# One conversion of 1024 columns for two neighbouring weight halves in a retention and two-layer feed-forward kernel

## The chip, the cores and the metric

The kernel runs on one core of a Trainium2 chip. The metric is the device time of one execution in microseconds; a median is taken over several executions. TensorE does the matrix products, ScalarE (ACT) and VectorE (DVE) everything elementwise, GpSimd (POOL) a little at the start, and SyncE (SP) issues nearly all transfers.

## What is computed

The reference, cut to what matters (2304 tokens, model width 512, hidden widths 1536 and 2048):

```python
scores = scale * q @ k.T
x = (scores * Dmat) @ v                      # decayed causal scores, 4 x 8 heads, 576 tokens
xn = x / sqrt(mean(x * x) + 1e-6) * rms_g    # first feed-forward block
g, val = xn @ w_gate, xn @ w_val
x = (g * sigmoid(g) * val) @ w_out
h = x @ w_in                                 # second feed-forward block
g = where(h >= 1, h, where(h <= -1, 0, (h + 1) ** 2 / 4))
out = g @ w_out2
```

## The kernel before, in words

**Three stages.** The attention stage works in chunks of 128 tokens (`scores` and `values`). The first feed-forward block follows: 36 steps (`step_a`), three blocks of 768 tokens with 12 steps of 128 hidden units each. The second block has three token blocks, each with eight front pieces (`front_b`) and a back part (`back_b`). Products are done as three matmuls on operands split into a rounded high and a low part (`split`: a ScalarE copy, then a VectorE subtraction), and each 2 by 2 block product takes seven products in place of eight, with sums of weight blocks and of token blocks made beforehand.

**The weights** come in as 64-bit numbers. `convert` (line 388) makes float32 of them. Its source is a ring of three buffers (`STAGE = 3`, laid out in line 345) in the tile `plain`; each holds one slot of 512 columns of 64 bits per partition, 512 KB, loaded by `load_slot` (line 380) on SP's queue. The three buffers lie side by side, so buffers 0 and 1 are neighbours, and 1 and 2; 2 and 0 are not. For each half of 512 columns, `convert` does a Prelu on ScalarE (upper words into the target), an Identity on ScalarE (the top byte of the lower words, with the bias `half`, into the stage buffer itself) and a scalar_tensor_tensor on VectorE that shifts and joins both; then it issues one `load_slot`, the refill of the ring. In program order both Preludes stand first, then Identity, join and refill of one half, then those of the other.

**Who calls it.** `prepare_a(s)` does a pair (gate and value weights, two slots) and then a single one (the output weights, one slot) for each of 12 steps; each is prepared one step ahead, the first two beside attention. `prepare_b` does one pair for each of 16 units (eight pieces, front and back weights) beside the steps from the 13th on that stand in `PREPARE`. After a pair comes the making of four sums on VectorE and `split_seven`, seven splits in three groups. In the 13th step and after, weights of the first block are read back from memory (`load_a`, tile `wt`; `load_out`), and those of the second are written out (`wfd`, `wod`, tile `late`) and read back later.

**The order** of the work is made by a planner (`Plan`). Every operation is recorded with its regions, a cost by a formula (`cost`), and a due time worked back from its users. `issue` then orders each engine's list: the operation ready next, and of those ready within 100 ns the one due first. TensorE keeps its program order. The order is fixed when the program is made, and each engine and SP's queue run it strictly in that order on the chip. In gaps of TensorE that the plan expects before 95 us it puts filler matmuls (line 1067). So a change of a few operations changes costs and may change the order of others on ScalarE, VectorE and SP.

Of the kernel before, what the change touches and what calls it, by code (L numbers as in the profile page):

```python
# [12 lines left out]
U32 = mybir.dt.uint32  # L13
# [7 lines left out]
NT, DM, FA, FB = B * S, H * D, 1536, 2048  # L21
# [9 lines left out]
TB = 384  # L31
SB = 2 * TB
NSB = NT // SB
NPB = NB // 2
# [4 lines left out]
STAGE = 3  # L39
# [267 lines left out]
def moe_chain_kernel(ctx: ExitStack, tc: tile.TileContext, att, tail, wa, wb, dmat, gq, gk, out):  # L307
# [6 lines left out]
    cut = lambda a, n: [a[:, i:i + n] for i in range(0, a.shape[-1], n)]  # L314
# [16 lines left out]
    plain = sb("plain", 6 * NPB * TB)  # L331

    def lay(a, at, *sizes):
        got = []
        for n in sizes:
            got.append(a[:, at:at + n])
            at += n
        return got
# [4 lines left out]
        plain, 0, 2 * KD * TB, NT, DM, 8 * DM, 3 * DM, CH + NPAIR * S, 2 * NPAIR * P  # L343
    )
    stages = lay(plain, 5 * NPB * TB, *[2 * DM] * STAGE)
    stages = [a.bitcast(U32).rearrange("p (a b) -> p a b", b=2) for a in stages]
    wpairs[1], w32o[1] = pieces[:, :2 * DM].bitcast(U32), pieces[:, 2 * DM:3 * DM]
    w32o = [a.bitcast(U32) for a in w32o]

# [28 lines left out]
    stage_t, loaded, taken, limit = {}, [0], [0], [3 * NA]  # L378

    def load_slot():  # L380
        i = loaded[0]
        if i < limit[0]:
            st = stages[i % STAGE]
            nc.sync.dma_start(out=st.rearrange("p a b -> p (a b)"), in_=slots[i].bitcast(U32))
            stage_t[i] = st
            loaded[0] += 1

    def convert(w):

        n = w.shape[-1] // DM  # L390
        while loaded[0] < taken[0] + n:
            load_slot()
        parts = []
        for q in cut(w, DM):
            st = stage_t.pop(taken[0])
            taken[0] += 1
            parts.append((q, st))
            nc.scalar.activation(
                out=q.bitcast(F32), in_=st.bitcast(F32)[:, :, 1], func=ACTF.Prelu, scale=2.0 ** -112, alpha=-(2.0 ** 32)
            )  # L400
        for q, st in parts:
            low = st.bitcast(U8).rearrange("p n (w b) -> p n w b", w=2)[:, :, 0, 3]
            nc.scalar.activation(out=st[:, :, 0], in_=low, func=ACTF.Identity, scale=2.0 ** -5, bias=half)
            nc.vector.scalar_tensor_tensor(
                out=q, in0=q, scalar=3, in1=st[:, :, 0], op0=ALU.logical_shift_left, op1=ALU.bitwise_or
            )
            load_slot()

    def convert_pair():
        j = SET[min(taken[0] // 3, NA)]  # L410
        w, sums = wpairs[j], wsums[j]
        convert(w)
        return w.bitcast(F32), sums
# [35 lines left out]
    def prepare_a(s):  # L449
        wa_t[s] = prepare_front(wts[s % 2])  # L450
        w = w32o[SET[s]]
        convert(w)
# [682 lines left out]
```

## Time and profile before

| | us |
|---|---|
| median of 3 runs | 855.52 (854.8 to 858.37) |
| profiled execution | 856.0 |
| its span | 854.2 |
| mean granted TensorE clock | 0.999 |
| busy: TensorE / VectorE / ScalarE / GpSimd | 846.9 / 675.1 / 565.6 / 53.6 |

The profiled execution's own time stands 1.8 us above its span (what lies around the first and the last instruction) and 0.5 us above the median. Busy time is the union of an engine's instructions; TensorE's includes filler matmuls and the ends of matmuls are modelled, so waits of its weight loads are looked at as well. All operations are recorded through one helper, so their line is L141, and the groups are told apart by tiles.

### The profile page before, as it was taken

The page shows a single profiled execution, that of the slowest core. Times are in us where ns is not written, and L with a number is a line of the kernel's source. Part 1 is how long each engine was busy: PE and PEld are TensorE (multiplying, and loading weights), DVE is VectorE, ACT ScalarE, POOL GpSimd, SP SyncE. Part 2 cuts the span into 40 slices and gives each one's busy share as a digit, 9 for nine tenths or more (in the row PEclk, how much of TensorE's full clock was granted, in tenths as well). Part 3 has the DMA queues.
Part 4 walks back from the last instruction along what each step waited for, and adds up shares of the span by engine and source line. Part 5 has one row for each costly group of instructions (what it writes and reads, how often), then busy time and mean ns, then how long its engine had stood idle before and what let it go on. Part 6 is the DMA issues. An engine that isn't in the chain of part 4 may idle for free.

```text
span 854.2 us, 14441 instructions
## 1 busy us (share of the span) xinstructions
PE 846.9 (99%) x5288; PEld 808.1 (95%) x5288; DVE 675.1 (79%) x1089; ACT 565.6 (66%) x1024; POOL 53.6 (6%) x64
## 2 busy tenths in 40 slices
PE   9999999999999999999999999999999999999997
PEld 8888999999999889999999999999999999999997
DVE  4888988889978888988698885798757789477854
ACT  4656888878567577866577777756367655477552
POOL 4776000000000000000000000000000000000000
PEclk9999999999999999999999999999999999999999
DMA  9994788787599988699899979999987789974685
GB/s 361 331 312 141 248 269 264 253 271 256 178 314 363 354 312 292 214 318 352 307 312 364 338 232 360 370 323 336 281 276 256 270 284 305 302 254 138 201 272 145
DMA packets 128423, 241.97 MB, mean 283 GB/s; under 512 B 40288, under 2 KB 70112, under 8 KB 126304
## 3 DMA queue, kind: packets, MB, share of 16 engines
q1 hardware_dynamic: 127120, 240.48, 83.8%
q8 instruction: 42, 0.69, 0.3%
q10 hardware_dynamic: 1232, 0.56, 0.3%
q14 instruction: 29, 0.24, 0.1%
HBM read 183.33 MB, written 57.67 MB: 282 GB/s over the span
## 4 chain that ended last, share of the span: by engine, by line
PE 96%; DMA 3%; DVE 1%; ACT 0%; issue 0%; DVEq 0%
PE fr L141 41%; PE acc L141 36%; PE at L141 18%; DMA wfd<-late 1%; DMA plain<-in_wb_dram 1%; PE acc L1067 1%; DMA wt<-wfa 1%; DVE att L141 0%; ACT att L141 0%; ACT wt L141 0%; DVE wt L141 0%; DVE wpair L141 0%; DVE plain L141 0%; DVE ones L141 0%; DVEq L141 0%
## 5 line engine op out<-in xcount | busy, mean ns | idle before, releaser
L141 PE MATMUL fr<-xall,wt 128*128 128x384 f32 x2016 | 400.2, 337 | 1.0 <-ACT att L141 0.6
L141 PEld LDWEIGHTS fr<-xall,wt 128*128 128x128 f32 x2016 | 356.2, 188 | 20.2 <-DVE att L141 2.4
L141 PE MATMUL acc<-rounded 128*128 128x512 f32 (+1 forms) x696 | 168.2, 369 | 0.0
L141 PEld LDWEIGHTS acc<-rounded 128*128 128x128 f32 x696 | 126.2, 188 | 8.4
L141 DVE TENSOR_TENSOR att<-fr,att 128x384 f32<-128x384 f32 x144 | 78.8, 555 | 37.6 <-PE fr L141 19.2
L141 ACT ACTIVATE att<-att 128x384 f32<-128x384 f32 x168 | 86.5, 524 | 30.2 <-DVE att L141 29.0
L141 ACT COPY att<-fr 128x384 f32<-128x384 f32 x144 | 68.9, 478 | 54.0 <-PE fr L141 52.6
L141 ACT CAST rounded<-plain 128x768 fp32r<-128x768 f32 (+1 forms) x68 | 54.3, 799 | 41.8 <-PE at L141 20.7
L141 DVE TENSOR_TENSOR rounded<-plain,rounded 128x768 fp32r<-128x768 f32 (+1 forms) x68 | 61.6, 906 | 18.5 <-ACT rounded L141 17.8
L141 PE MATMUL at<-rounded 128*128 128x512 f32 (+1 forms) x288 | 75.5, 376 | 0.0
L141 DVE TENSOR_TENSOR plain<-plain 128x768 f32<-128x768 f32 (+1 forms) x84 | 66.2, 805 | 3.3 <-DMA plain<-x2d 2.6
L141 DVE SCALAR_TENSOR_TENSOR plain<-att,plain 128x384 f32<-128x384 f32 x72 | 39.3, 552 | 25.5 <-ACT att L141 25.4
L141 DVE TENSOR_TENSOR wt<-wt 128x768 fp32r<-128x768 f32 (+1 forms) x48 | 52.0, 1084 | 7.9 <-ACT wt L141 7.9
L141 PE MATMUL acc<-xall,wt 128*128 128x384 f32 x288 | 57.8, 335 | 0.0
L141 ACT ACTIVATE att<-plain 128x384 f32<-128x384 f32 x72 | 37.8, 525 | 27.8 <-DVE plain L141 27.7
L141 ACT CAST wt<-wt 128x768 fp32r<-128x768 f32 (+1 forms) x48 | 45.2, 944 | 15.4 <-DMA wt<-wfa 15.4
L141 PEld LDWEIGHTS at<-rounded 128*128 128x128 f32 x288 | 52.4, 187 | 3.0
L141 ACT ACTIVATE plain<-plain,half 128x512 uint32<-128x512 uint8 x68 | 51.9, 767 | 0.0
L141 PEld LDWEIGHTS acc<-xall,wt 128*128 128x128 f32 x288 | 50.6, 188 | 0.0
L141 PE MATMUL acc<-late,rounded 128*128 128x384 f32 x264 | 50.6, 335 | 0.0
L141 PE MATMUL acc<-rounded,late 128*128 128x384 f32 x264 | 49.8, 335 | 0.0
L141 PEld LDWEIGHTS acc<-late,rounded 128*128 128x128 f32 x264 | 46.3, 188 | 0.0
(105 smaller groups left out, 1104.8 us busy)
## 6 DMA issues: line engine op xcount, KB each, us to landing
rounded<-wod SPq DMA_DIRECT2D x56, 512.0 KB, 5.1
wt<-wfd SPq DMA_DIRECT2D x48, 512.0 KB, 5.1
plain<-in_wa_dram SPq DMA_DIRECT2D x36, 512.0 KB, 5.0
wt<-wfd SPq DMA_DIRECT2D x24, 768.0 KB, 4.9
plain<-in_wb_dram SPq DMA_DIRECT2D x32, 512.0 KB, 6.4
late<-wod SPq DMA_DIRECT2D x28, 512.0 KB, 5.2
att<-in_att_dram SPq DMA_DIRECT2D x26, 512.0 KB, 5.7
wt<-wfa SPq DMA_DIRECT2D x24, 512.0 KB, 6.0
```

The source lines that it names most:

```text
L141: getattr(real, method)(*[fresh(a) for a in args], **{k: fresh(a) for k, a in kwargs.items()})
L1067: nc.keep_warm = lambda bank: tc.nc.tensor.matmul(bank, lhsT=ones, rhs=ones, start=True, stop=True)
```

## The change

Where a pair's two slots lie in neighbouring buffers (the first in buffer 0 or 1), Prelu, Identity and join are one operation each over 1024 columns, on a view `pairs[at]` over both buffers; the two refills are issued after the join. Where the first slot lies in buffer 2, and for the single slots of the output weights, all stays as before.

```diff
     stages = lay(plain, 5 * NPB * TB, *[2 * DM] * STAGE)
-    stages = [a.bitcast(U32).rearrange("p (a b) -> p a b", b=2) for a in stages]
+    pairs = [plain[:, 5 * NPB * TB + i * 2 * DM:5 * NPB * TB + (i + 2) * 2 * DM] for i in range(STAGE - 1)]
+    stages, pairs = ([a.bitcast(U32).rearrange("p (a b) -> p a b", b=2) for a in g] for g in (stages, pairs))
...
         parts = []
-        for q in cut(w, DM):
+        at = taken[0] % STAGE
+        wide = n == 2 and at + 1 < STAGE
+        for q in [w] if wide else cut(w, DM):
             st = stage_t.pop(taken[0])
             taken[0] += 1
+            if wide:
+                stage_t.pop(taken[0])
+                taken[0] += 1
+                st = pairs[at]
             parts.append((q, st))
...
-            load_slot()
+            for _ in range(n if wide else 1):
+                load_slot()
```

## Rows read from the trace of the kernel before

**Rows 1.** The page: busy times, and the granted clock in 40 slices.

```profile
PE 846.9 (99%) x5288; PEld 808.1 (95%) x5288; DVE 675.1 (79%) x1089; ACT 565.6 (66%) x1024; POOL 53.6 (6%) x64
...
PEclk9999999999999999999999999999999999999999
```

**Rows 2.** Busy time by stretch, columns as the first line says.

```profile
core 0: us, PE busy (x) PEld busy (x) DVE busy (x) ACT busy (x) POOL busy (x), PEclk, DMA share, GB/s
0.00:20.00 20.00, 18.95 (x226) 17.66 (x227) 9.04 (x18) 10.15 (x27) 7.80 (x14) 1.00 0.93 358
...
80.00:100.00 20.00, 19.78 (x109) 18.40 (x108) 16.57 (x32) 16.61 (x32) 1.54 (x4) 1.00 0.56 173
...
140.00:160.00 20.00, 20.00 (x106) 18.78 (x105) 17.78 (x33) 16.42 (x30) 0.00 (x0) 1.00 0.83 267
...
260.00:280.00 20.00, 19.88 (x105) 18.33 (x104) 17.94 (x33) 13.41 (x25) 0.00 (x0) 1.00 1.02 369
280.00:300.00 20.00, 19.51 (x100) 17.23 (x98) 15.72 (x26) 13.29 (x24) 0.00 (x0) 1.00 0.96 350
...
800.00:854.00 54.00, 48.92 (x283) 48.59 (x281) 32.35 (x42) 19.79 (x27) 0.00 (x0) 0.98 0.74 214
```

**Rows 3.** Waits of TensorE's weight loads, whole span: total us, times, longest.

```profile
PEld fr L141 <- DVE att L141: 2.4, 8, 0.5
PEld fr L141 <- ACT att L141: 2.2, 4, 0.9
```

**Rows 4.** Groups by shape: busy us, mean ns of one, idle before.

```profile
L141 ACT ACTIVATE plain<-plain,half 128x512 uint32<-128x512 uint8 x68 | 51.9, 767 | 0.0
...
L141 ACT ACTIVATE wpair<-plain 128x512 f32<-128x512 f32 x44 | 29.2, 670 | 2.5 <-DMA plain<-in_wa_dram 1.5 <-DVE wsum L141 0.7
...
L141 DVE SCALAR_TENSOR_TENSOR wpair<-wpair,plain 128x512 uint32<-128x512 uint32 x44 | 30.0, 684 | 1.9 <-ACT plain L141 1.6
...
L141 DVE TENSOR_TENSOR wt<-plain,wt 128x1024 fp32r<-128x1024 f32 x6 | 7.3, 1214 | 0.0
...
L141 ACT CAST wt<-plain 128x1024 fp32r<-128x1024 f32 x6 | 6.3, 1048 | 0.4 <-DVE plain L141 0.4
...
L141 DVE TENSOR_TENSOR wt<-plain,wt 128x512 fp32r<-128x512 f32 x6 | 4.1, 685 | 0.1
...
L141 ACT CAST wt<-plain 128x512 fp32r<-128x512 f32 x6 | 3.7, 617 | 0.0
```

**Rows 5.** VectorE's timeline, 250 to 302 us: the joins of two units.

```profile
273.40 0.68 DVE L141 SCALAR_TENSOR_TENSOR wpair<-wpair,plain 128x512 uint32<-128x512 uint32 x1
...
274.94 0.68 DVE L141 SCALAR_TENSOR_TENSOR wpair<-wpair,plain 128x512 uint32<-128x512 uint32 x1
...
289.44 0.68 DVE L141 SCALAR_TENSOR_TENSOR wpair<-wpair,plain 128x512 uint32<-128x512 uint32 x1
...
292.11 0.68 DVE L141 SCALAR_TENSOR_TENSOR wpair<-wpair,plain 128x512 uint32<-128x512 uint32 x1
```

**Rows 6.** SP's timeline, 250 to 302 us: refills and the next weight load.

```profile
274.11 1.92 SPq L141 DMA_DIRECT2D plain<-in_wb_dram  x2
276.98 0.38 SPq L141 DMA_DIRECT2D wt<-wfa  x1
```

**Rows 7.** ScalarE's timeline, 250 to 302 us: what that load holds up.

```profile
280.69 1.05 ACT L141 CAST wt<-wt 128x1024 fp32r<-128x1024 f32 x1 [3.04 <-DMA wt<-wfa]
281.64 0.47 ACT L141 COPY att<-fr 128x384 f32<-128x384 f32 x1
```

**Rows 8.** Waits of all engines, 85 to 220 us: ScalarE on the slots' loads.

```profile
ACT plain L141 <- DMA plain<-in_wa_dram: 2.1, 5, 0.6
ACT wpair L141 <- DMA plain<-in_wa_dram: 1.5, 1, 1.5
```

**Rows 9.** Groups by shape: the filler matmuls.

```profile
L1067 PE MATMUL acc<-ones 128*128 128x128 f32 x56 | 8.0, 282 | 0.0
```

**Rows 10.** ScalarE, the tile `plain` from 480 us: the last Identities.

```profile
L141 ACT ACTIVATE plain<-plain,half x2: 764/768/773, 495.1 to 500.2; 128x512 uint32<-128x512 uint8 x2
```

## The prediction

> **What bounds the kernel now.** I read the page first. TensorE is busy for 846.9 of 854.2 us, VectorE for 79% and ScalarE for 66%, and the granted clock is full in all 40 slices [rows 1]. The reader is to see that only the 7.3 us in which TensorE isn't busy can be given back, except for filler.
>
> The stretches say where these lie [rows 2]. The end holds 54 − 48.92 = 5.1 us and the first 20 us hold 1.05. Between them only three 20 us stretches concern us: 0.22 at 80, 0.12 at 260 and 0.49 at 280, together 0.83 us. In a typical stretch of the first feed-forward block, at 140, TensorE is busy for 20.00 of 20 us, although VectorE already stands at 17.78.
>
> Ends of matmuls are modelled, so I took the waits of TensorE's weight loads too. They waited 2.4 us for VectorE's and 2.2 us for ScalarE's evacuations of partial products [rows 3], 4.6 us in all. This is the larger figure for what late elementwise work costs TensorE, and I use it as the bound.
>
> Last I followed one late evacuation back. At 280.69 ScalarE starts a cast of weights after waiting 3.04 us for their load; a copy that frees a partial product stands behind it and runs at 281.64 [rows 7]. That load went out on SP's queue at 276.98, behind two refills of the ring begun at 274.11 [rows 6]. The transfer engines show a share of 1.02 and 0.96 in these stretches [rows 2]. So the stalls that exist near 260 to 300 us come from a weight load that lands late, not from ScalarE having too much to do.
>
> **The change part by part.** How many pairs become wide follows from the positions. The first block takes three slots a step, so its 12 pairs all begin in buffer 0. The 16 units of the second block begin in buffers 0, 2, 1 in turn; five begin in 2 and stay, 11 become wide. That makes 23 wide pairs, the last beside the last Identities at 500.2 us [rows 10].
>
> *ScalarE.* Before, a pair takes 2 × 670 = 1340 ns of Prelu and 2 × 767 = 1534 ns of Identity [rows 4]. No row shows either at 1024 columns. The nearest are the casts, 617 ns at 512 columns and 1048 at 1024 [rows 4]: 431 ns for 512 more. That gives 670 + 431 = 1101 and 767 + 431 = 1198, a saving of 239 + 336 = 575 ns a pair, 13.2 us for 23. The other end is that twice the columns take twice as long, which saves nothing; a loss is excluded, as both 1024-column rows cost less than two of 512. I take 13.2, from the rows nearest in engine and size.
>
> *VectorE.* The join takes 684 ns. The subtractions take 685 at 512 columns and 1214 at 1024, so a wide join takes about 684 + 529 = 1213, against 1368: 155 ns a pair, 3.6 us for 23, between 0 and 3.6 as above.
>
> *What these are worth.* Both savings lie beside TensorE. In the first block's early steps TensorE has no idle time to give back [rows 2], so the 12 pairs there are worth nothing in time; the cover is TensorE's own work. The two prepared beside attention could shorten a gap there. Gaps are filled with 56 matmuls, 8.0 us busy in all [rows 9], and a pair saves 0.16 us of VectorE, so I put 2 × 0.16 = 0.3 us on this at most and 0 in the sum. For the 11 later pairs the end of the gain is the 4.6 us of weight-load waits, if all of them fell to ScalarE's and VectorE's load. I take 0, because the one followed back was a transfer's.
>
> *The wait that is added.* A wide Prelu waits for both slots. In the program both Preludes stood ahead of the rest, and the second had to wait for its slot as well. What moves is the first Prelu's 670 ns, behind that wait. ScalarE waited for slots 2.1 + 1.5 = 3.6 us in the first block's early steps [rows 8], while TensorE stayed full at 140. Queued behind it on ScalarE are the evacuating copies and SiLUs. It costs 0 while slots land early; otherwise at most 12 × 0.67 = 8.0 us in the first block, if every one came late, which these waits speak against.
>
> *Longer operations.* A copy that frees a partial product may stand behind 1101 or 1198 ns of ScalarE where it stood behind 670 or 767, and VectorE's sum behind 1213 in place of 684: 0.4 to 0.5 us more. Casts of 1048 and subtractions of 1214 ns are in every step already [rows 4], and TensorE is full with them. I take 0; as the price of a bad placement, 0.5 us for each of 23 pairs on one engine is 11.5 us at the far end.
>
> Here a page speaks against the change. The Trainium skill, Perfetto Trace Analysis, section Optimizing Scalar/DVE Operations, says that grouping helps where the engine is saturated, and that breaking up instructions can help where Scalar and Vector aren't saturated but cause bubbles on other engines. Neither condition is clear in these rows; by the first the sum would be as in the faster rival below, by the second as in the slower.
>
> *The refills.* The number of transfers stays, 36 and 32 of 512 KB. What moves is when SP may issue them: before, the first after the first join, now both after the wide one. In the unit at 273 us the second join begins 274.94 − 273.40 = 1.5 us after the first, in the one at 289 us 292.11 − 289.44 = 2.7 us [rows 5]. So the first refill goes out 1.5 to 2.7 us later; the second about as now, since the three operations take 1101 + 1198 + 1213 = 3.5 us, and the old chain to the second join's end 2 × 670 + 2 × 767 + 684 = 3.6. SP runs in order, so a weight load planned behind the first refill waits too. In the unit at 273 us both refills already stand ahead of the weight load, 1.92 us for the two and then 276.98. The transfer engines are full there, so the bytes ahead of that load are the same and I put 0 on it. With the cover of a full transfer queue gone, the price is the whole 1.5 to 2.7 us. POOL's queue isn't passed by anything.
>
> *The sum.* 856.0 us of the profiled execution, minus 0 and plus 0, is 856.0. It stands 0.5 us above the median of the runs, so against that median I forecast 855.5 us. What goes off ScalarE and VectorE turns into their idle time. The planner works with new costs, so the order of other work shifts too; I allow 2 us either way for that, about half of the waits that its present order leaves.
>
> **The rivals.** *Faster: evacuations come earlier.* If the 4.6 us of weight-load waits come from ScalarE and VectorE being crowded, 16.8 us less work there takes all of them away, and with 0.3 us beside attention the time is 855.5 − 4.9 = 850.6 us. For it: the waits name these engines. Against it: the followed one began with a transfer, and most of the saving falls where TensorE is full.
>
> *Slightly faster: VectorE as good as saturated.* At 17.78 of 20 us VectorE is nearly full in the first block's early steps. If it set the pace there, 12 × 155 ns = 1.9 us would come off: 853.6 us. Against it: TensorE is idle for 0.00 us in that stretch.
>
> *Slower: the late refill.* SP holds weight loads behind a refill that waits for the wide join; their casts land late on ScalarE, and copies stand behind them. Its place is the units between 240 and 320 us, of which four become wide, and the price of each is the slip of the first refill, 1.5 to 2.7, on average 2.1 us: 8.4 us. The wait of 3.04 us cost TensorE no more than the 0.49 us idle of its stretch, so 2.5 us are hidden; in a queue that runs in order the slips add up, and the cover counts once. That gives 855.5 + 8.4 − 2.5 = 861.4 us. It decides from the point at which the transfer engines run empty during the slip and the delays pass 2.5 us. For it: a wait of 3.04 us already reaches TensorE. Against it: a share of 0.96 to 1.02.
>
> *The change doesn't do what it says* can't take more than the five pairs that begin in buffer 2; with none wide the time would be 855.5 all the same.
>
> **How the numbers follow.** About 0.5% (4.3 us) is what a measurement of this kernel can tell from no change, so faster means below 851.2 and slower above 859.8. I give the forecast 0.76, the slightly faster case 0.07 (both within the bound), the faster rival 0.05 and the slower one 0.12. This gives 0.05, 0.83, 0.12. The range takes the 2 us of the order, goes down to 852.5 to take in the slightly faster case, and up to 859.8, over half the way to the slower rival; it leaves out about 0.15.
>
> **What would show it.** Right: 45 Identities in place of 68, 23 of them near 1200 ns; ScalarE's busy time down by some 13 us and VectorE's by 3 to 4; TensorE idle for about 7 us again, most of it at the end. Wrong: Preludes or Identities near twice their old length; weight-load waits near 0 (the faster rival) or above 10 us with longer waits of ScalarE's casts for `wt` between 240 and 320 us (the slower); a full clock no longer granted; another number of filler matmuls. A different order around 20 to 90 us, with TensorE stalled there, would overturn the sum without any of the named mechanisms.

## The result and the profile after

The changed kernel takes 862.2 us against 855.88 us, a ratio of 1.0057 (95% interval 1.0038 to 1.0077). The profiled execution took 861.95 us, its span 860.2: 6.0 us more than before. The forecast was 855.5 us and no difference; this lies above the range.

The page's busy times after, to be held against [rows 1]:

```profile
PE 849.2 (99%) x5282; PEld 806.4 (94%) x5282; DVE 674.7 (78%) x1066; ACT 561.4 (65%) x980; POOL 53.9 (6%) x64
```

ScalarE is busy for 4.2 us less and VectorE for 0.4 us less. TensorE isn't busy for 860.2 − 849.2 = 11.0 us in place of 7.3, and its busy time, in which the modelled ends of matmuls hide short waits, grew too. The stretches show where, the first line naming the columns as in [rows 2]:

```profile
core 0: us, PE busy (x) PEld busy (x) DVE busy (x) ACT busy (x) POOL busy (x), PEclk, DMA share, GB/s
...
80.00:100.00 20.00, 18.80 (x101) 16.59 (x98) 16.30 (x26) 17.13 (x27) 2.56 (x4) 1.00 0.42 134
100.00:120.00 20.00, 19.28 (x101) 17.40 (x100) 18.76 (x35) 15.48 (x28) 0.00 (x0) 1.00 0.81 251
...
140.00:160.00 20.00, 19.78 (x103) 17.86 (x102) 17.95 (x32) 14.76 (x25) 0.00 (x0) 1.00 0.79 256
...
260.00:280.00 20.00, 19.46 (x102) 17.85 (x101) 15.68 (x27) 13.07 (x23) 0.00 (x0) 1.00 1.02 364
280.00:300.00 20.00, 20.00 (x106) 18.59 (x105) 17.50 (x27) 14.04 (x22) 0.00 (x0) 1.00 0.89 310
300.00:320.00 20.00, 19.52 (x101) 17.75 (x100) 15.92 (x27) 12.74 (x22) 0.00 (x0) 1.00 0.85 275
...
480.00:500.00 20.00, 19.68 (x102) 17.86 (x101) 14.79 (x23) 13.86 (x23) 0.00 (x0) 1.00 0.87 330
...
800.00:860.20 60.20, 54.84 (x317) 54.52 (x315) 37.01 (x49) 23.36 (x33) 0.00 (x0) 0.98 0.72 209
```

TensorE is idle for 1.20 us at 80, where it was 0.22, and for 0.72, 0.22 and 0.32 us at 100, 140 and 480, where it was never idle. The 0.49 us at 280 are gone; at 260 the idle time grew from 0.12 to 0.54 us, at 300 from 0.13 (left out by the prediction) to 0.48. The granted clock stays at its full level up to the end stretch (1.00 in all rows above but the last). The end costs 60.2 − 54.84 = 5.4 us, about as before.

The waits of TensorE's weight loads, against [rows 3]:

```profile
PEld fr L141 <- DVE att L141: 5.1, 11, 0.8
PEld fr L141 <- ACT att L141: 4.7, 12, 0.8
```

9.8 us in place of 4.6, for the same work: evacuations of partial products come later, often by a few tenths of a microsecond.

The groups by shape, against [rows 4] and [rows 9], and the table loads (the last line is the kernel before):

```profile
L141 ACT ACTIVATE plain<-plain,half 128x1024 uint32<-128x1024 uint8 x23 | 28.4, 1236 | 0.0
L141 DVE SCALAR_TENSOR_TENSOR wpair<-wpair,plain 128x1024 uint32<-128x1024 uint32 x17 | 20.8, 1223 | 6.4 <-ACT plain L141 6.3
L141 ACT ACTIVATE wpair<-plain 128x1024 f32<-128x1024 f32 x17 | 19.5, 1145 | 0.9 <-DMA plain<-in_wb_dram 0.7
...
L1075 PE MATMUL acc<-ones 128*128 128x128 f32 x50 | 7.3, 283 | 0.0
...
L141 ACT ACT_TABLE_LOAD x4 | 5.1, 1283 | 2.2 <-issue 2.2
```

```profile
L141 ACT ACT_TABLE_LOAD x2 | 2.6, 1283 | 2.2 <-issue 2.2
```

All 23 pairs became wide. The operations are nearly as short as estimated: 1145, 1236 and 1223 ns for 1101, 1198 and 1213. But 17 wide joins waited 6.3 us for their Identities, where 44 narrow ones waited 1.6 us [rows 4]. And ScalarE loads an activation table four times in place of two. The filler matmuls are 50 in place of 56, one of the signs of being wrong that the prediction named: the plan expects other gaps, so its order is another.

To see where the loss arises I counted off the 42 matmuls of each step on the banks `fr` in both traces and subtracted the times at which a step's first one starts (us, later than in the kernel before; "block 2" is the third front piece of the second block):

```
step             0      1      2     13     24     30     35   block 2
changed      -0.03  +0.74  +3.50  +2.78  +3.57  +3.15  +6.76  +5.93
```

About 2.8 us go between 90 and 103 us, and some 3 us more between 425 and 500 us. The first place is the seam between attention and the first block. ScalarE's timeline there, before and after:

```profile
84.70 1.06 ACT L141 ACTIVATE plain<-acc,eps 128x256 f32<-128x256 f32 x2
...
88.10 1.28 ACT L141 ACT_TABLE_LOAD   x1
```

```profile
81.17 1.22 ACT L141 ACTIVATE plain<-plain,half 128x1024 uint32<-128x1024 uint8 x1
...
85.80 0.47 ACT L141 ACTIVATE plain<-acc,eps 128x256 f32<-128x256 f32 x1 [1.06 <-PE acc L141]
...
87.88 1.28 ACT L141 ACT_TABLE_LOAD   x1
...
91.72 1.28 ACT L141 ACT_TABLE_LOAD   x1
93.02 0.69 ACT L141 ACTIVATE plain<-acc,eps 128x512 f32<-128x512 f32 x1
...
97.57 1.28 ACT L141 ACT_TABLE_LOAD   x1
```

The rows named `plain<-acc,eps` are reciprocal square roots (x2 at 84.70: both); the table at 87.88 is for the SiLUs. Before, both roots stood ahead of the only table load in this stretch. In the new order the root of 512 columns comes behind the first SiLU, so the table goes back and forth: two more loads of 1.28 us. The kernel's own guard (the first SiLU is planned behind the Square of the 256 columns) doesn't cover the other root.

The second place is the end of the first block. From 424 to 502 us ScalarE's casts into the tile `late` have to wait until a store from it has landed (before, then after):

```profile
ACT late L141 <- DMA wfd<-late: 0.7, 1, 0.7
ACT late L141 <- DMA wfd<-late: 5.2, 4, 1.9
```

In three of the four cases a copy that frees a partial product stands right behind the cast. One of them, on ScalarE and TensorE:

```profile
484.20 1.05 ACT L141 CAST late<-wsum 128x1024 fp32r<-128x1024 f32 x1 [1.84 <-DMA wfd<-late]
485.16 0.47 ACT L141 COPY att<-fr 128x384 f32<-128x384 f32 x1
485.68 1.32 PE L141 MATMUL fr<-xall,wt 128*128 128x384 f32 x6 [0.33 <-ACT att L141]
```

No run took these waits alone away, so their share of the 3 us isn't shown.

One thing ahead of the prediction needs correction. It says that TensorE keeps its program order; the planner prefers it only among operations that are nearly ready. So TensorE's order moved too. Its timeline before and after:

```profile
90.01 4.46 PE L141 MATMUL fr<-xall,wt 128*128 128x384 f32 x24
```

```profile
90.75 2.38 PE L141 MATMUL fr<-xall,wt 128*128 128x384 f32 x12 [0.25 <-DVE att L141]
92.97 0.39 PE L141 MATMUL acc<-rounded 128*128 128x512 f32 x1
```

### The profile page after: what moved, and what is told of

The parts are those of the page before. It is cut to its first block, busy times and chain, and to the rows that moved or that the text cites. A ratio compares the mean times of both kernels' runs of the same rounds, so it can differ in the third digit from the quotient of the medians.

```text
span 860.2 us, 14359 instructions
## 1 busy us (share of the span) xinstructions
PE 849.2 (99%) x5282; PEld 806.4 (94%) x5282; DVE 674.7 (78%) x1066; ACT 561.4 (65%) x980; POOL 53.9 (6%) x64
## 4 chain that ended last, share of the span: by engine, by line
PE 87%; DMA 8%; ACT 2%; DVE 2%; issue 1%; POOL 0%; ACTq 0%; POOLq 0%; SPq 0%; DVEq 0%
PE fr L141 36%; PE acc L141 33%; PE at L141 17%; DMA wt<-wfa 3%; DMA plain<-in_wa_dram 1%; DMA plain<-x2d 1%; DMA wfd<-late 1%; DMA plain<-in_gq_dram 1%; ACT plain L141 1%; DMA x2d<-plain 1%; DVE att L141 1%; PE acc L1075 0%; POOL plain L141 0%; DVE wt L141 0%; DVE plain L141 0%
## 5 line engine op out<-in xcount | busy, mean ns | idle before, releaser
L141 ACT COPY att<-fr 128x384 f32<-128x384 f32 x144 | 68.7, 477 | 57.9 <-PE fr L141 56.3
L141 PE MATMUL at<-rounded 128*128 128x512 f32 (+1 forms) x288 | 79.3, 376 | 0.2 <-ACT rounded L141 0.2
L141 PEld LDWEIGHTS acc<-rounded,late 128*128 128x128 f32 x264 | 46.3, 188 | 0.0
```

Source lines behind the costliest of these rows:

```text
L141: getattr(real, method)(*[fresh(a) for a in args], **{k: fresh(a) for k, a in kwargs.items()})
```

## The experiments

Ratios are to the kernel before, run on the same chip. The theories: A, the order that the planner makes from the wide operations is worse; B, the refills go out late (the slower rival); C, a long operation stands in front of evacuations; later D, the two more table loads make the first loss; E, the coarser conversions themselves make it.

### The two blocks apart

```diff
-        wide = n == 2 and at + 1 < STAGE
+        wide = n == 2 and at + 1 < STAGE and taken[0] < 3 * NA     # e1; >= in e2
```

> Wide only in the 12 pairs of the first block; the 16 units of the second block as before. Theory A (two separate losses: two additional activation table loads of 1.28 us each near 92 and 98 us, with TensorE some 3 us late from there on, and another 3 us in the second block's units between 255 and 500 us): four table loads in the trace, and about 3 us over the kernel before, near 859 us. Theory B (the units' late refills alone make all of it): no different from the kernel before, near 856 us. Theory C (long operations stand in front of evacuations wherever they are): the loss spreads with the 12 of 23 pairs, near 859 us, but grows from 90 to 215 us instead of standing still after 105 us.

> Wide only in the 11 units of the second block; the 12 pairs of the first block as before. Theory A: two table loads as before the change, TensorE in step with the kernel before up to 240 us, then 3 us lost up to 500 us, near 859 us. Theory B: the whole loss, near 862 us. Theory C: near 859 us.

The first block alone: 1.0024 (1.0012 to 1.0036). The second alone: 1.0047 (1.0029 to 1.0065). In the first run's trace TensorE loses 3.6 us up to step 2, with four table loads, and then stays 3.2 to 6.0 us late without the steady growth that C needs. In the second run's trace it stays level with the kernel before to 240 us (+0.8 us throughout, from the start-up), and goes from 0.3 us early at step 30 to 3.6 us late at step 35. So there are two separate losses, as A said, and B can't be all of it. The parts add up to 0.71%, not 0.57%; the intervals allow both.

### One table load taken away

```diff
+        if b == 2:
+            nc.ops[last][2].add(last - 3)      # in rms: Square of 256 behind Square of 512
```

> The changed kernel with one dependency more in the plan: the last reciprocal square root of 256 columns also waits for the Square of the 512 columns, so both reciprocal square roots come ahead of the first SiLU. Theory A: two table loads, TensorE about 0 to 1 us late at 105 us in place of 3.5, near 859 us. Theory B and C: the table loads aren't what costs; near 862 us.

1.0059 (1.0038 to 1.0080), with two table loads: no time came back. A was wrong here. The order was made anew, and other waits took the place: TensorE is 3.0 us late at step 2 (1.1 of it from the start-up), where the changed kernel is 3.5, and 4.0 at step 3. Its longest stall comes after that, on ScalarE and then TensorE:

```profile
155.60 1.12 ACT L141 ACTIVATE plain<-plain 128x1024 f32<-128x1024 f32 x1 [3.25 <-DMA wfa<-plain]
156.63 0.51 ACT L141 ACTIVATE att<-att 128x384 f32<-128x384 f32 x1
157.04 0.46 ACT L141 COPY att<-fr 128x384 f32<-128x384 f32 x1
157.56 1.34 PE L141 MATMUL fr<-xall,wt 128*128 128x384 f32 x6 [1.37 <-ACT att L141]
```

The wide Prelu overwrites a pair that is still being stored; ScalarE stands for 3.25 us, the copy that frees a partial product stands behind it, and TensorE is idle for 1.37 us.

### The order held, the width changed

First the changed kernel's order, with each wide operation issued as two:

```diff
+    def in_halves(w, both, kind):
...
+            for i in range(2):
+                q, st = w[:, i * DM:(i + 1) * DM], both[:, i * DM:(i + 1) * DM]
...
+            if wide:
+                in_halves(q, st, 0)
```

> The order of the changed kernel, made with its costs, but each wide operation is issued as two of 512 columns in its place. Theory A (the order that the planner makes is the cause, not the length of an operation): four table loads, near 862 us, as the changed kernel. Theory C (the length): near 856 us. If the length makes only the second loss: near 859 us.

1.0041 (1.0024 to 1.0059). Most of the loss stays without a single wide operation on the chip, four table loads among it, and at the same two places: TensorE loses 2.8 us from step 1 to step 2 and 4.9 us from step 30 to step 35. Both refills still stand behind the second join here, so this run alone doesn't part the order from B. Its weight loads wait as long as the changed kernel's:

```profile
PEld fr L141 <- ACT att L141: 5.9, 12, 1.7
PEld fr L141 <- DVE att L141: 4.7, 12, 0.7
```

Then the reverse: the order of the kernel before, each pair issued wide in the place of the second half. The first half is skipped, and what needs it and stood ahead of the wide operation comes right behind it.

```diff
-            ops[i][1]()
+            if i in self.merged:
+                continue
+            if not give(i):
...
+                    nc.merged[i] = j, lambda: at_once(kind, w, pairs[at])
```

> The plan is made with the narrow operations, so the order of the kernel before; each pair's two operations are then issued as one of 1024 columns in the place of the second, and what needs it follows it. Theory A (the order that the planner makes from the wide operations is the cause): two table loads and no loss, 0 to 1 us from the kernel before. Theory C (an operation of 1.2 us stands in front of evacuations): the loss stays, 5 to 6 us over the kernel before. Theory B (refills go out late, here too): most of the loss stays in the second block, some 3 us over.

1.0322 (1.0304 to 1.0340), 27 us over. Far worse than any theory said. The mean granted clock was 0.994 to 0.997 in these executions, against 0.998 to 1.000 in the kernel before, so some 3.5 us of this may be the clock (an estimate: 0.4% of 884 us, with TensorE taken as busy throughout). The waits of this run (line 423 is the wide join, 421 the wide Identity), then ScalarE's and VectorE's timeline of one pair:

```profile
PEld fr L142 <- DVE att L142: 15.9, 22, 2.3
DVE wpair L423 <- ACT plain L421: 13.3, 12, 1.6
PEld fr L142 <- ACT att L142: 13.0, 16, 2.3
```

```profile
96.50 1.14 ACT L417 ACTIVATE wpair<-plain 128x1024 f32<-128x1024 f32 x1
97.54 1.22 ACT L421 ACTIVATE plain<-plain,half 128x1024 uint32<-128x1024 uint8 x1
...
98.79 1.23 DVE L423 SCALAR_TENSOR_TENSOR wpair<-wpair,plain 128x1024 uint32<-128x1024 uint32 x1 [1.54 <-ACT plain L421]
```

VectorE stands for 1.54 us until the whole Identity is done, and evacuations queue behind it. In the kernel before, VectorE joined this pair's first half ahead of the second half's Identity, and ScalarE was already casting joined weights:

```profile
93.41 0.69 DVE L141 SCALAR_TENSOR_TENSOR wpair<-wpair,plain 128x512 uint32<-128x512 uint32 x1
...
94.40 0.61 ACT L141 CAST wt<-wpair 128x512 fp32r<-128x512 f32 x1
94.91 0.77 ACT L141 ACTIVATE plain<-plain,half 128x512 uint32<-128x512 uint8 x1
```

The last run of this group holds the place and takes the width away; both halves are issued in the place of the second:

```diff
+    def at_once(kind, w, both):
+        for q, st in zip(cut(w, DM), cut_both(both)):
+            one_half(kind, q, st)
```

> As the run with the old order and wide operations (3.2% slower), but in the place of the second operation both halves are issued one after the other, 512 columns each. If the place is what costs (the first half's work comes as late as the second's, so VectorE no longer joins one half while ScalarE works on the other), nearly the same loss, 20 us or more; if the length of 1024 columns costs, no more than a few us over the kernel before.

1.0182 (1.0140 to 1.0223), from four executions, the longest (877.77 us) at a granted clock of 0.990. So of the 3.2%, about 1.8% come from bringing the first half's work, and its refill, to the second's time, and the rest, about 1.4%, from the width on top. Neither forecast was right alone. Its waits lie between:

```profile
PEld fr L142 <- DVE att L142: 12.2, 20, 1.6
DVE wpair L430 <- ACT plain L428: 9.2, 10, 1.4
PEld fr L142 <- ACT att L142: 6.1, 11, 2.0
```

### Parts of the step, and an order made anew without it

```diff
+            if True and wide:                       # e6: narrow, both refills behind the second join
+                floor, nc.floor = nc.floor, len(nc.ops) - 1
                 load_slot()
+                load_slot()
...
+        for p in both if True else halves:          # e8: Prelu alone wide
+            prelu(*p)
...
+            for p in both:                          # e18: join alone wide, refills behind it
+                join(*p)
...
-RATE, LAND, ISSUE, LANES = 370, 3000, 380, 8
+RATE, LAND, ISSUE, LANES = 372, 3000, 380, 8        # e7: kernel before, planned with another rate
```

> Narrow operations as before; only the two refills of a pair that lies in neighbouring buffers both wait for the second join, in the plan and on the chip. Theory A (any coarser step makes a worse plan): 2 to 4 us over the kernel before, lost between 80 and 150 us. Theory B (late refills hold up transfers and so the weights' casts): 5 to 6 us over, most of it from 240 us on. Theory C (length): no different from the kernel before.

> The kernel before, planned with a transfer rate of 372 in place of 370 bytes per ns and nothing else: the same operations in an order made anew. If any new order costs several us (the order before is a lucky one), 3 to 6 us over the kernel before. If the wide operations make the order worse, under 1 us over.

> Only the Prelu of a neighbouring pair is one operation of 1024 columns; Identity, join and refill stay in halves, each refill behind its own join. Theory A (any coarser step makes a worse plan): 4 to 7 us over the kernel before, part of it near 100 us. Theory B (late refills): no different from the kernel before. Theory C: a third of the loss at most, under 2 us.

> Only the join of a neighbouring pair is one operation of 1024 columns, with both refills behind it; Prelu and Identity stay in halves. Theory A (the first half's results come later, and the order that is made from it is worse): 2 to 4 us over the kernel before. Theory C: a third of the loss, under 2 us.

Late refill: 1.0060 (1.0033 to 1.0087), but its ten executions fall apart, and the granted clock with them: five from 857.6 to 859.5 us at 0.997 to 0.999, five from 864.6 to 866.9 us at 0.990 to 0.994. The median lies between the two groups; that of the five short ones is 1.5 us over the kernel before. The profiled execution (858.8 us) is 2.3 us late at step 0 already, with a granted clock of 0.93 from 40 to 60 us, and no later at step 35, so no loss shows where B puts it; where the clock fell in the longer executions wasn't profiled. Another rate: 1.0017 (1.0003 to 1.0032). Prelu alone: 1.0022 (1.0010 to 1.0035), join alone: 1.0022 (1.0009 to 1.0034). So the merged Prelu and the merged join each cost by themselves no more than an order made anew for no reason, and the Prelu's run has four table loads besides. The Identity alone was not run. The order made anew at another rate also has 50 filler matmuls in place of 56.

### Pairs picked out

```diff
+        wide = ... and (taken[0] == 0 or taken[0] >= 60)   # e9: four pairs
+        wide = ... and taken[0] == 3                       # e10: the second pair; e14: with e3's dependency
+        wide = ... and 3 < taken[0] < 3 * NA               # e15: the ten pairs from the third on
+        wide = ... and 3 * NA <= taken[0] < 50             # e16: the first seven units
+            nc.ops[after_rms - 4][2].add(len(nc.ops) - 1)  # e13: kernel before, one root behind the SiLU
```

> Wide only in four pairs: the first of all, which is made beside attention, and the last three of the second block that lie in neighbouring buffers. Two table loads in the plan, as before. Theory A (a wide operation costs only where the order made from it puts it in the way): no different from the kernel before, within 1.5 us. Theory C (the length costs wherever it stands): 4 of 23 pairs, 1 us.

> Wide only in the second pair of the first block, the one made at the seam between attention and the first steps. Four table loads in the plan. Theory A: this pair alone makes the step near 90 to 100 us that the changed kernel shows, 2 to 3.5 us over the kernel before, though it takes three operations away. Theory C: 0.25 us.

> The kernel before, narrow, with one dependency that puts the reciprocal square root of 512 columns behind the first SiLU, so that two table loads more are made; no wide operation. Theory D (the two loads, 2 x 1.28 us, stand in TensorE's way): 2.5 to 3.5 us over the kernel before, lost by 105 us. Theory E (ScalarE has room for them there and the coarser conversions cost elsewhere): under 1 us over.

> Only the second pair wide, with the dependency that keeps both reciprocal square roots ahead of the first SiLU: two table loads. Theory D: no different from the kernel before, so its 2.8 us were the loads. Theory E: 2 to 3 us over, as without the dependency.

> Wide in the ten pairs of the first block from the third on; two table loads. Theory D: no different from the kernel before, within 1 us, as this stretch has no such load. Theory E: 3 to 4 us over, as the twelve pairs together, lost between 90 and 160 us where the pairs' results are due.

> Wide in the five of the first seven units of the second block that lie in neighbouring buffers. The eleven cost 0.47%. If those that share the stretch of 240 to 350 us with the full transfer queue make it (the late refill), 3 us or more over; if the units from the eighth on do, or the three last, under 1 us.

Four pairs: 1.0008 (0.9996 to 1.0020), no difference that can be told. The second pair alone: 1.0032 (1.0020 to 1.0045), the time that A forecast, but in the trace TensorE loses only 1.3 us of it up to step 2; with the table loads kept to two, 1.0021 (1.0006 to 1.0036). D forecast no difference for the latter and missed, and the two intervals overlap. The tables alone, all narrow: 1.0029 (1.0014 to 1.0044), 859.26 against 856.7 us, 2.6 us, as much as 2 × 1.28 us (the interval allows 1.2 to 3.8); of it TensorE loses 2.1 us between step 0 and step 3. Ten pairs of the first block: 1.0070 (1.0043 to 1.0096). That is more than all twelve cost (1.0024), and it has two table loads only; two wide pairs fewer made it slower. Its longest stall has the cause of the one above, though TensorE is 3.7 us late at step 3 already, ahead of it. ScalarE and TensorE in this run:

```profile
144.85 1.13 ACT L141 ACTIVATE wpair<-plain 128x1024 f32<-128x1024 f32 x1 [2.31 <-DMA wfa<-wpair]
145.88 0.47 ACT L141 COPY att<-fr 128x384 f32<-128x384 f32 x1
146.40 1.31 PE L141 MATMUL fr<-xall,wt 128*128 128x384 f32 x6 [1.70 <-ACT att L141]
```

The first seven units, five of them wide: 1.0023 (1.0007 to 1.0039), so about half of what the eleven cost; the rest comes with the later ones, though the last three alone were free.

### Looking less far ahead

```diff
-    HOLD, COLD = 100, 4000
+    HOLD, COLD = 10, 4000       # e11: kernel before; e12: changed kernel, 0
```

> The kernel before, narrow, with the planner looking 10 ns ahead in place of 100 when it chooses among operations that are nearly ready; nothing else. If the order decides and its plan is nearer to what the chip does, 1 to 2 us faster than the kernel before; if this figure only moves noise, within 1 us of it.

> The changed kernel, all 23 pairs wide, planned without looking ahead; two table loads. Theory A: another order gives a part of the loss back, 2 to 4 us over the kernel before in place of 6. Theory C (length, in any order): 6 us over it still.

1.0025 (1.0011 to 1.0039) and 1.0084 (1.0059 to 1.0109). Both missed: neither beats the kernel before, and the changed one got no better (its interval overlaps that of 1.0057). No version that was tried beats the kernel before.

## Why the prediction was wrong

**The bound and the prices of the operations were right.** TensorE bounds the kernel, 23 pairs became wide, and the wide operations took within 4% of the estimates. That none of this gives time back was right as well.

**The busy times fell by less than the sum.** I forecast 13 us for ScalarE and 3 to 4 for VectorE; the page shows 4.2 and 0.4. Added up one by one over both traces, ScalarE's instructions take 9.1 us less (612.8 for 621.9): 11.6 us less for the operations and 2.6 us more for two table loads. But neighbours overlap (in the new timeline a Prelu starts at 94.91 and lasts 1.13 us, and the next operation starts at 95.95), the page counts such time once, and with fewer instructions there are 4.9 us less of it (51.4 for 56.3). That leaves the 4.2. On VectorE it is 2.1 us less, and 1.7 us less overlap. The sum took durations for busy time.

**The step that failed is the order.** "I allow 2 us either way for that", says the sum. The runs show this term to be the larger part of the effect, and on one side: the new order without any wide operation costs 0.41% (e4), 3.5 us, of the 0.57%, and at the same two places. Even an order made anew from the same narrow operations costs 0.17 and 0.25% (e7, e11). Two orders are few, but both are slower, so no run supports an estimate centred on zero. The place was named ("a different order around 20 to 90 us, with TensorE stalled there, would overturn the sum") and given no chance of its own.

**The chain of a conversion was summed in series.** I wrote 3.5 us against 3.6 and concluded that the second half ends as before. With the measured durations the sum is 1145 + 1236 + 1223 ns = 3.6 us, so for the three operations that holds. But the halves were a pipeline of two engines, and the first half's join was done before ScalarE came to the second half's Identity. I priced this for the refill alone. What it is worth with the order held: about 1.8% for the first half's delay, its refill's included, and 3.2% with the width (e17, e5). An order made anew takes most of it back, and what it moves costs then: a root behind a SiLU, and an operation in front of a store that hasn't landed (the casts into `late` in the changed kernel, the Preludes of e3 and e15).

**Longer operations in front of evacuations: "I take 0".** The trace had 1048 and 1214 ns operations in every step, and I took that as proof that there was room for more. In the old order there was not: width alone adds about 1.4% (e17 to e5). In the new order, narrow in place of wide gives back the difference between 1.0057 and 1.0041, whose intervals overlap, so a price of the width isn't shown there.

**The rivals.** The slower one had the sign and, at 861.4 us, nearly the time, but not the place. Its sign was longer waits of ScalarE's casts for `wt` between 240 and 320 us; they waited 6.8 us in both kernels (before, then after):

```profile
ACT wt L141 <- DMA wt<-wfa: 6.8, 7, 3.0
ACT wt L141 <- DMA wt<-wfa: 6.8, 8, 1.8
```

And most of the loss lies outside 240 to 320 us (+2.78 at step 13, +3.57 at step 24). So its time was near by luck, as far as these runs show. The later waits for stores also begin with a transfer, but from 424 us on and not for these loads. Whether late refills have a part in them stays open: the profiled execution of e6 loses 0.7 us between step 30 and step 35, and its executions spread too far to tell.

**What spoke against the change.** TensorE's weight loads did wait for evacuations of VectorE and ScalarE, 4.6 us before and 9.8 after, with neither engine saturated (busy for 78% and 65% of the span). The Trainium skill, Perfetto Trace Analysis, section Optimizing Scalar/DVE Operations, says that breaking up instructions may allow work to be completed sooner in this case. Joining them did the opposite, and the trace agrees in the sign; but most of the loss stayed when the new order was issued in halves (e4), so the size isn't shown to come from this.

**What stays open.** Why one order is better than another isn't reduced to a single wait. It was two table loads in one run, single waits for stores in two others, and in the changed kernel table loads at the seam, waits for stores at the end of the first block and many short waits; what each of these costs there isn't shown. The loss isn't a sum over pairs (ten cost more than twelve), so no price per wide pair can be given.

## What to carry to other kernels

Where an automatic schedule with strict queues already keeps the bounding engine full, an edit off the critical path is judged by the order that comes out of it: compare the two orders, look for table switches and for operations at the head of a queue that wait for a transfer, and hold the order fixed in one run to tell the edit from the schedule. Two halves that pass from one engine to the next are a pipeline; joining them saves fixed cost on both engines and takes the overlap away. When a plan has a guard against a costly order (here the table switch), check that it covers every operation that can break it.

## What was not expected of the hardware

Two more switches of the activation table cost 2.6 us in time (e13; the interval allows 1.2 to 3.8), about the 1283 ns of each load. In the timeline of the changed kernel nothing stands beside the load: the one at 91.72 follows an operation that ends at 91.70 and is followed by one at 93.02.

```profile
91.19 0.51 ACT L141 CAST rounded<-att 128x384 fp32r<-128x384 f32 x1
```

The Trainium skill, ScalarE: Activation LUTs, section What ACT_TABLE_LOAD costs, gives about 1283 ns for the load, which agrees, and about 1380 ns of drain beside it, which these rows don't show.

An operation that overwrites a tile while a store from it is under way waits until the store has landed, and on ScalarE's queue the evacuations behind it wait as well: 3.25 us in e3, 2.31 us in e15, 1.84 us in the changed kernel, of which TensorE was idle for 1.37, 1.70 and 0.33 us.
